# A 448-column first tile, one row for both signs, and a newly searched order in a fused Fourier and SwiGLU kernel

## The chip, the cores and the metric

The kernel runs on one core of a Trainium2 chip. The core has five engines that run side by side, each with its own queue of instructions: TensorE (PE, matrix products into the PSUM banks), VectorE (DVE) and ScalarE (ACT), which read and write PSUM and SBUF, GpSimd (POOL), which works on SBUF, and SyncE (SP), which here issues DMAs. They wait for each other by semaphores. The metric is the time of one execution in microseconds of device time. A profile shows one execution; its *span* runs from its first to its last instruction.

## The reference, cut to what matters

```python
def _attn_ref(x):                       # x: [8, 3008, 256]
    X = np.fft.fft(x, axis=1)           # along the sequence
    X = np.fft.fft(X, axis=2)           # along the features
    return X.real.astype(np.float32)

def _moe_ref(x, w_gate, w_val, w_out):  # x: [24064, 256]; w_gate, w_val: [256, 1536]; w_out: [1536, 256]
    g = x @ w_gate
    silu = g * (1.0 / (1.0 + np.exp(-g)))
    val = x @ w_val
    return (silu * val @ w_out).astype(np.float32)
```

The real part of a two-dimensional Fourier transform of each of eight batches is the token matrix of a gated feed-forward block: two projections to 1536 features, SiLU of the one times the other, and a projection back to 256.

## The kernel before, in words

**Pairs of rows.** Rows k and 3008 - k of a transformed batch share their cosine part P and have sine parts Q of opposite sign. So the kernel works on half the rows, 1504 columns for each of eight batches, 12,032 in all, and makes two results of each column: a *plus* value from P and Q, and a *minus* value with Q's sign turned. The eight rows 0, which have no partner, are eight more plus columns of the last tile. The transform along the features is folded into the weights: Wp and Wq are the weights for P and Q, and Wm is -2 Wq, so adding Wm times Q to a finished plus sum turns it into the minus sum.

**Tiles and units.** The columns are cut into 24 tiles (`wide`, line 41) of 512 columns, but for tiles 0 and 3 with 480 and the last with 320. T is 512, P is 128, H is 1504 columns a batch. A *unit* is a tile and one of twelve blocks of 128 of the 1536 features. `part_a` (line 1123) makes the plus sums of gate and value in PSUM banks g and v, `part_b` (line 1179), one unit later, the minus sums and the products. The plus product goes to the tile `hp`, the minus product to `hm` (`tiles_of`, line 1045), both bf16, the minus one in mirrored column order.

**Kinds.** `KINDS` (line 989) has one character for each unit, which says who does what. `w` is a whole unit: six matmuls, plus and minus sums from Wp, Wq and Wm, silus on ACT, both products on DVE; tile 0 has only these, since they need no prepared row. For the others the character is a hexadecimal number of flags. Without flags a unit has five matmuls: gate from Wp, Wq and Wm, value from Wp and Wq, and DVE makes the minus value as twice the even part less the plus sum. Flag 2 saves the gate's Wm matmul in the same way, for two more DVE instructions. Flag 1 lets ACT put the row-0 correction into the value bank ahead of time (a *seed*) and copy the even part, in place of a DVE instruction; that value then takes Wm as its last matmul. Flag 4 gives the plus product to POOL, whose instructions here read SBUF only, so ACT first copies the value to SBUF (`pp`, line 1250). Flag 8 gives POOL the minus value too (line 1256). The minus products of two units always go to POOL in one instruction (line 1244).

**Output blocks.** `OWork` (line 1269) multiplies the products of the tile before by Wo, in blocks of up to 128 columns: twelve matmuls for a block, one for each feature block, with the block as the weights that are loaded and the 256 columns of Wo streaming. Two blocks share a PSUM bank; ACT copies a pair to SBUF (`evict`), in one instruction where both have 128 rows and in two otherwise, and SP stores it, in as many pieces as the row order of the output asks for. Before the change the blocks of one sign are cut separately, so that a 480-column tile has blocks of 128, 128, 128 and 96 for each sign. The very last pair is evicted to an `es` buffer and stored from ACT's queue.

**Order.** Nothing runs in the order in which the program text makes it. Each operation goes to a planner (`Sched`, line 828) with an estimated duration, a due time on PE's own clock and the buffers that it takes and frees; the planner sets the order of every engine's queue before the kernel is built. The due time is shifted by `SHIFT` for each sort of operation and by `BIAS_ROWS` (line 778; the table above it is overwritten) for each tile and sort. The Fourier work of the next batches (folds on POOL, transform products on PE whose sums DVE writes to the tiles of P and Q) and of the weights (line 1519 with casts on ACT and DVE) is mixed in at fixed unit numbers, the main loop begins at line 1695.

Of the kernel before, what the change touches and what calls it, by code (L numbers as in the profile page):

```python
# [19 lines left out]
def kernel(  # L20
# [20 lines left out]
    wide = [H - 2 * T, T, T] * 2  # L41
# [674 lines left out]
    def rows(r0, n, step):  # L716
# [60 lines left out]
    )  # L777
    BIAS_ROWS = (
# [202 lines left out]
    def pool_us(n):  # L981
# [9 lines left out]
        "60ww24000310",  # L991
        "031310330010",
        "000031313300",
        "010210121013",
        "10110b103101",
        "031305121252",
        "401700014001",
        "331213050030",
        "010271031001",
        "33040b350300",  # L1000
        "01b300700101",
        "21302111b200",
        "001371310011",
        "23520011b212",
        "10130b130000",
        "031035003170",
        "013370040411",
        "303b21011210",
        "103b10219604",
        "0030b13300b0",  # L1010
        "616404563200",
        "143034169230",
        "704161632331",
# [31 lines left out]
    def tiles_of(t):  # L1045
        if t not in hts:
            hts[t] = (hp.tile([P, nF, T + B], BF16, name="hp"), hp.tile([P, nF, T], BF16, name="hm"))
        return hts[t]

# [73 lines left out]
    def part_a(u):  # L1123
# [9 lines left out]
        def h():  # L1133
            if t not in hts:
                hts[t] = (hp.tile([P, nF, T + B], BF16, name="hp"), hp.tile([P, nF, T], BF16, name="hm"))

# [42 lines left out]
    def part_b(u):  # L1179
# [15 lines left out]
        def sv():  # L1195
            if ksv not in T_:
                T_[ksv] = svp.tile([P, 2, T, 2], F32, name="sv")
            return T_[ksv]

        def hts_(t):  # L1200
            if t not in hts:
                hts[t] = (hp.tile([P, nF, T + B], BF16, name="hp"), hp.tile([P, nF, T], BF16, name="hm"))
            return hts[t]

        def g3():
            if by_dve:
                mm(T_[kg], Wq, 0, u, pq_tiles(t)[1], wp, False, True)
            else:
                mm(T_[kg], Wm, 0, u, pq_tiles(t)[1], w, False, True)

# [32 lines left out]
        def product_m():  # L1243
            nc.gpsimd.tensor_tensor(hts_(t)[1][:, f - 1:f + 1, :w], sv()[:, :, :w, 1], sv()[:, :, :w, 0], op=Alu.mult)  # L1244

        def product_p():
            nc.vector.tensor_tensor(hts_(t)[0][:, f, :wp], T_[ksp][:, :wp], T_[kv][:, :wp], op=Alu.mult)  # L1247
# [395 lines left out]
    def row_width(t):  # L1643
        return width(t) + (B if t == nT - 1 else 0)
# [138 lines left out]
```

## Time and profile before

| | |
|---|---|
| runs | 597.38, 598.56, 598.67 us; median 598.56 |
| profiled execution, span (the page gives no other time for it) | 596.2 us |
| PE busy | 590.3 us, 99% |
| DVE busy | 569.2 us, 95% |
| ACT busy | 553.6 us, 93% |
| POOL busy | 533.1 us, 89% |
| granted clock of PE | 1.000 |
| moved by DMA | 68.17 MB |

A row of a group reads: line, engine, operation, output<-inputs with shapes, count, then busy time, mean duration of one in ns, and the idle time of the engine just before with what ended it. A row of the timeline reads: start, duration, engine, line, what, count, and in brackets an idle time before it. A row of waits reads: who waited, for whom, total us, times, longest. Records of matmuls overlap, and those of ACT and DVE a little, so a duration can be longer than the distance between two starts. L1033 is the line of all gate and value matmuls, L1297 of the output matmuls.

### The profile page before, as it was taken

The page shows a single profiled execution, that of the slowest core. Times are in us where ns is not written, and L with a number is a line of the kernel's source. Part 1 is how long each engine was busy: PE and PEld are TensorE (multiplying, and loading weights), DVE is VectorE, ACT ScalarE, POOL GpSimd, SP SyncE. Part 2 cuts the span into 40 slices and gives each one's busy share as a digit, 9 for nine tenths or more (in the row PEclk, how much of TensorE's full clock was granted, in tenths as well). Part 3 has the DMA queues.
Part 4 walks back from the last instruction along what each step waited for, and adds up shares of the span by engine and source line. Part 5 has one row for each costly group of instructions (what it writes and reads, how often), then busy time and mean ns, then how long its engine had stood idle before and what let it go on. Part 6 is the DMA issues. An engine that isn't in the chain of part 4 may idle for free.

```text
span 596.2 us, 12375 instructions
## 1 busy us (share of the span) xinstructions
PE 590.3 (99%) x4001; PEld 388.7 (65%) x4001; DVE 569.2 (95%) x1063; ACT 553.6 (93%) x1071; POOL 533.1 (89%) x491
## 2 busy tenths in 40 slices
PE   8999999999999999999999999999999999999997
PEld 5456666666666666666666666666666666666686
DVE  8989999999999999999999999999999999999993
ACT  8768989999999899999999999999999999999995
POOL 8989999999999999999899998999889868687782
PEclk9999999999999999999999999999999999999999
DMA  8966772756243255275225122063121103202212
GB/s 244 166 219 234 189 230 71 195 165 220 83 151 126 70 144 132 54 254 165 81 79 171 37 63 64 19 182 113 47 63 37 47 19 89 66 29 63 60 54 81
DMA packets 61086, 68.17 MB, mean 114 GB/s; under 512 B 6760, under 2 KB 48684, under 8 KB 61022
## 3 DMA queue, kind: packets, MB, share of 16 engines
q1 hardware_dynamic: 57438, 64.44, 36.1%
q0 software_dynamic: 3216, 2.36, 2.8%
q8 instruction: 31, 0.51, 0.4%
q10 hardware_dynamic: 368, 0.59, 0.3%
q14 instruction: 33, 0.27, 0.1%
HBM read 40.21 MB, written 35.43 MB: 127 GB/s over the span
## 4 chain that ended last, share of the span: by engine, by line
PE 95%; DMA 1%; POOL 1%; SPq 1%; DVE 0%; ACT 0%; issue 0%; ACTq 0%; POOLq 0%
PE o L1297 40%; PE g L1033 27%; PE v L1033 21%; PE g L1471 2%; PE o L1471 2%; PE v L1297 1%; DMA XC<-in_x_dram 1%; DMA out_dram<-ev 1%; PE o L1519 1%; POOL t L373 0%; PE g L628 0%; PE o L628 0%; SPq L1310 0%; PE b L502 0%; PE b L490 0%
## 5 line engine op out<-in xcount | busy, mean ns | idle before, releaser
L1244 POOL TENSOR_TENSOR hm<-sv 128x1024 bf16<-128x1024 f32 (+2 forms) x137 | 254.7, 1862 | 32.7 <-ACT sv L1220 16.8
L1236 DVE SCALAR_TENSOR_TENSOR sv<-es,v 128x512 f32<-128x512 f32 (+2 forms) x262 | 174.5, 672 | 6.2 <-PE v L1033 4.3
L1297 PE MATMUL o<-Wo,hm 128*128 128x256 bf16 (+1 forms) x1128 | 163.7, 273 | 0.0
L1297 PE MATMUL o<-Wo,hp 128*128 128x256 bf16 (+1 forms) x1104 | 161.1, 272 | 0.0
L1247 DVE TENSOR_TENSOR hp<-sp,v 128x512 bf16<-128x512 f32 (+2 forms) x228 | 152.0, 673 | 1.8 <-PE v L1033 1.0
L1297 PEld LDWEIGHTS <-hm 128*128 128x128 bf16 (+2 forms) x1140 | 111.9, 98 | 58.0 <-issue 0.6
L1297 PEld LDWEIGHTS <-hp 128*128 128x128 bf16 (+2 forms) x1140 | 111.9, 98 | 55.4 <-issue 0.6
L1220 ACT ACTIVATE sv<-g 128x512 f32<-128x512 f32 (+2 forms) x181 | 118.4, 672 | 3.7 <-PE g L1033 3.2
L1145 ACT ACTIVATE sp<-g 128x512 f32<-128x512 f32 (+2 forms) x181 | 111.6, 618 | 6.1 <-PE g L1033 4.5
L1033 PE MATMUL g<-Pt,Wp 128*128 128x512 bf16 (+2 forms) x288 | 107.5, 374 | 0.0
L1033 PE MATMUL v<-Pt,Wp 128*128 128x512 bf16 (+2 forms) x288 | 106.2, 374 | 0.0
L1033 PE MATMUL g<-Qt,Wq 128*128 128x512 bf16 (+2 forms) x288 | 105.4, 375 | 0.0
L1106 ACT ACTIVATE v<-bc,w 128x512 f32<-128x512 bf16 (+2 forms) x139 | 99.7, 721 | 1.7 <-DVE sv L1236 0.9
L1170 DVE SCALAR_TENSOR_TENSOR es<-bc,w,v 128x512 f32<-128x512 bf16 (+2 forms) x135 | 98.1, 734 | 2.1
L1168 ACT ACTIVATE es<-v 128x512 f32<-128x512 f32 (+2 forms) x139 | 85.4, 617 | 3.3 <-PE v L1033 1.5
L1033 PE MATMUL g<-Qt,Wm 128*128 128x512 bf16 (+2 forms) x195 | 73.1, 376 | 0.0
L1033 PEld LDWEIGHTS <-Wp 128*128 128x128 bf16 x576 | 56.3, 98 | 25.2 <-issue 0.3
L1149 DVE SCALAR_TENSOR_TENSOR sg<-bc,w,g 128x512 f32<-128x512 bf16 (+2 forms) x93 | 67.5, 726 | 1.6 <-PE g L1033 1.4
L1253 POOL TENSOR_TENSOR hp<-sp,pp 128x512 bf16<-128x512 f32 (+1 forms) x46 | 57.1, 1245 | 8.0 <-ACT pp L1250 7.8
L1220 ACT ACTIVATE sv<-sg 128x512 f32<-128x512 f32 (+2 forms) x93 | 63.4, 693 | 0.5 <-POOL hp L1253 0.5
L1213 DVE SCALAR_TENSOR_TENSOR sg<-sg,g 128x512 f32<-128x512 f32 (+2 forms) x93 | 61.8, 665 | 0.2
L1033 PEld LDWEIGHTS <-Wq 128*128 128x128 bf16 x437 | 42.7, 98 | 28.4 <-issue 1.3
(201 smaller groups left out, 781.8 us busy)
## 6 DMA issues: line engine op xcount, KB each, us to landing
out_dram<-ev SPq DMA_DIRECT2D x96, 128.0 KB
XA<-in_x_dram SPq DMA_DIRECT2D x30, 256.0 KB
tA<-in_x_dram SPq DMA_DIRECT2D x28, 256.0 KB
XA<-tA SPq DMA_DIRECT2D x14, 512.0 KB
XC<-in_x_dram SPq DMA_DIRECT2D x28, 120.0 KB
tC<-in_x_dram SPq DMA_DIRECT2D x28, 120.0 KB
XC<-tC SPq DMA_DIRECT2D x6, 480.0 KB
bc<-br SPq DMA_DIRECT2D x19, 128.0 KB
```

What stands on the lines that cost most here:

```text
L1033: nc.tensor.matmul(ps[:, :n], Wt[:, gv, fs], src[:, :n], start=start, stop=stop, skip_group_check=True)
L1106: nc.scalar.activation(T_[kv][:, :w], bc[t][:, :w], AF.Copy, scale=w0[:, 1, f:f + 1])
L1145: nc.scalar.activation(sp_to()[:, :w], T_[kg][:, :w], AF.Silu)
L1149: nc.vector.scalar_tensor_tensor(T_[keg][:, :w], bc[t][:, :w], w0[:, 0, f:f + 1], T_[kg][:, :w], op0=Alu.mult, op1=Alu.add)
L1168: nc.scalar.activation(T_[kes][:, :w], T_[kv][:, :w], AF.Copy, scale=2.0 if on_pool(u) > 1 else 1.0)
L1170: nc.vector.scalar_tensor_tensor(T_[kes][:, :w], bc[t][:, :w], w0[:, 1, f:f + 1], T_[kv][:, :w], op0=Alu.mult, op1=Alu.add)
L1213: nc.vector.scalar_tensor_tensor(T_[kgm][:, :w], T_[keg][:, :w], 2.0, T_[kg][:, :w], op0=Alu.mult, op1=Alu.subtract)
L1220: nc.scalar.activation(sv()[:, f % 2, w - 1::-1, 1], T_[kgm if by_dve else kg][:, :w], AF.Silu)
L1236: nc.vector.scalar_tensor_tensor(sv()[:, f % 2, w - 1::-1, 0], T_[kes][:, :w], 2.0, T_[kv][:, :w], op0=Alu.mult, op1=Alu.subtract)
L1244: nc.gpsimd.tensor_tensor(hts_(t)[1][:, f - 1:f + 1, :w], sv()[:, :, :w, 1], sv()[:, :, :w, 0], op=Alu.mult)
L1247: nc.vector.tensor_tensor(hts_(t)[0][:, f, :wp], T_[ksp][:, :wp], T_[kv][:, :wp], op=Alu.mult)
L1297: nc.tensor.matmul(st["ps"][:n, j, :], hts[t][minus][:, f, c:c + n], Wo[:, f, :], start=(f == 0), stop=(f == nF - 1))
```

## The change

The first tile becomes 448 columns and all others but the last 512, so that tile 0 to 5 still cover two batches; the edge that was at column 1504, a batch's end, moves to 1472, and tile 3 now holds the last 32 columns of batch 0. Plus and minus products share one tile `h` of 1024 columns a feature block, the plus part first, and the minus part right behind it. Output blocks are cut over the whole row, so that a block can hold the end of the plus part and the start of the minus part; `stores` splits such a block by sign. A pair is evicted in two copies where one of its blocks is short, as before; in the last tile that is now the last pair, 128 and 8 rows. `KINDS` and `BIAS_ROWS` are replaced from the second tile on, the overwritten table is dropped, and three helpers that made the product tiles are merged into `tiles_of`.

```diff
-    wide = [H - 2 * T, T, T] * 2
+    wide = [2 * H - 5 * T] + [T] * 5
...
     BIAS_ROWS = (
         (8.55, -4.05, -3.45, 7.8, -31, -13.15, 16.6, 26.65, 26.15, 26.3, 26.75, 7.5, 3, 12.8, 13.35, -4.7, 4.55),
-        (-19.65, -7.75, -12.4, -1.6, -7, 5.65, -2.85, -2.85, 2.25, -3.5, 35.9, -0.75, -0.15, 1.9, -1.6, 3.8, -6.4),
...
+        (4.255, 1.638, -0.543, 4.143, -1.421, 1.089, -0.108, -0.795, -0.026, 0.763, 9.204, -7.067, -4.062, -1.119, -3.083, 5.491, -4.643),
...
     KINDS = (
         "wwwwwwwwwwww",
-        "60ww24000310",
-        "031310330010",
-        "000031313300",
-        "010210121013",
-        "10110b103101",
-        "031305121252",
-        "401700014001",
-        "331213050030",
-        "010271031001",
-        "33040b350300",
-        "01b300700101",
-        "21302111b200",
-        "001371310011",
-        "23520011b212",
-        "10130b130000",
-        "031035003170",
-        "013370040411",
-        "303b21011210",
-        "103b10219604",
-        "0030b13300b0",
-        "616404563200",
-        "143034169230",
-        "704161632331",
+        "20ww00001101",
+        "213013443211",
+        "013031130101",
+        "123010311010",
+        "131000950001",
+        "213103111213",
+        "012145214301",
+        "031772700001",
+        "301071033010",
+        "312154035212",
+        "503310b00011",
+        "329271130301",
+        "211044001071",
+        "630307142030",
+        "112147034000",
+        "039603903301",
+        "301013560400",
+        "377601444303",
+        "1b00592b7004",
+        "00922150b630",
+        "644b24124920",
+        "7073400b6000",
+        "70b27724b220",
     )
...
     def tiles_of(t):
         if t not in hts:
-            hts[t] = (hp.tile([P, nF, T + B], BF16, name="hp"), hp.tile([P, nF, T], BF16, name="hm"))
+            h = hp.tile([P, nF, 2 * T], BF16, name="h")
+            w = row_width(t)
+            hts[t] = (h[:, :, 0:w], h[:, :, w:w + width(t)], h)
         return hts[t]
+
+    def row_width(t):
+        return width(t) + (B if t == nT - 1 else 0)
...
             w = width(t)
-            blocks = []
-            for minus in (0, 1):
-                n = w + (B if (t == nT - 1 and not minus) else 0)
-                for c in range(0, n, P):
-                    blocks.append((minus, c, min(P, n - c)))
+            wp = row_width(t)
+            blocks = [(c, min(P, wp + w - c)) for c in range(0, wp + w, P)]
...
-            nc.tensor.matmul(st["ps"][:n, j, :], hts[t][minus][:, f, c:c + n], Wo[:, f, :],
+            nc.tensor.matmul(st["ps"][:n, j, :], hts[t][2][:, f, c:c + n], Wo[:, f, :],
                              start=(f == 0), stop=(f == nF - 1))
...
         def stores(self, pair, t):
-            return [(jj, p0, cnt, r0, step) for jj, (mi, cc, nn) in enumerate(pair)
-                    for p0, cnt, r0, step in row_pieces(t0[t] + (width(t) - cc - nn if mi else cc), nn, mi)]
+            w, wp = width(t), row_width(t)
+            res = []
+            for jj, (c, n) in enumerate(pair):
+                for lo, hi, minus in ((c, min(c + n, wp), 0), (max(c, wp), c + n, 1)):
+                    if lo < hi:
+                        first = wp + w - hi if minus else lo
+                        res += [(jj, lo - c + p0, cnt, r0, step) for p0, cnt, r0, step in row_pieces(t0[t] + first, hi - lo, minus)]
+            return res
```

Counted in the instruction orders of the two kernels, the totals over all tiles go as follows.

| | before | after |
|---|---|---|
| gate and value matmuls | 1361 | 1357 |
| output matmuls | 2280 | 2268 |
| units with flag 2 (gate split) | 93 | 97 |
| units with flag 1 (seed) | 139 | 137 |
| plus products on POOL | 46 | 67 |
| minus values on POOL | 12 | 15 |
| store issues on SP / ACT | 278 / 1 | 280 / 2 |

More of the change, by code (lines that the diff above doesn't have):

```diff
@@ L752 @@
     BIAS_ROWS = (
[24 rows of a table removed]
-    )
-    BIAS_ROWS = (
[24 rows of a table removed]
[24 rows of a table added]
     )
@@ L1131, in part_a @@
         kb = (("bc", t), 0)
-        def h():
-            if t not in hts:
-                hts[t] = (hp.tile([P, nF, T + B], BF16, name="hp"), hp.tile([P, nF, T], BF16, name="hm"))
         def g1():
@@ L1198, in sv @@
             return T_[ksv]
[L1200 to L1203, printed above, removed]
         def g3():
@@ L1243, in product_m @@
         def product_m():
-            nc.gpsimd.tensor_tensor(hts_(t)[1][:, f - 1:f + 1, :w], sv()[:, :, :w, 1], sv()[:, :, :w, 0], op=Alu.mult)
+            nc.gpsimd.tensor_tensor(tiles_of(t)[1][:, f - 1:f + 1, :w], sv()[:, :, :w, 1], sv()[:, :, :w, 0], op=Alu.mult)
         def product_p():
-            nc.vector.tensor_tensor(hts_(t)[0][:, f, :wp], T_[ksp][:, :wp], T_[kv][:, :wp], op=Alu.mult)
+            nc.vector.tensor_tensor(tiles_of(t)[0][:, f, :wp], T_[ksp][:, :wp], T_[kv][:, :wp], op=Alu.mult)
         def value():
@@ L1252, in product_g @@
         def product_g():
-            nc.gpsimd.tensor_tensor(hts_(t)[0][:, f, :wp], T_[ksp][:, :wp], pair_of(u)[:, :wp], op=Alu.mult)
+            nc.gpsimd.tensor_tensor(tiles_of(t)[0][:, f, :wp], T_[ksp][:, :wp], pair_of(u)[:, :wp], op=Alu.mult)
         def mirror_g():
@@ L1282, in __init__ @@
                 pair = blocks[i:i + 2]
-                if len(pair) == 2 and pair[0][0] != pair[1][0]:
-                    pair = pair[:1]
                 i += len(pair)
@@ L1289, in __init__, with product @@
                     st.update(home=(esp, "es"), queue=nc.scalar)
-                for j, (minus, c, n) in enumerate(pair):
+                for j, (c, n) in enumerate(pair):
                     for f in range(nF):
-                        self.steps.append((st, pair, j, minus, c, n, f, t))
-        def product(self, st, pair, j, minus, c, n, f, t):
+                        self.steps.append((st, pair, j, c, n, f, t))
+        def product(self, st, pair, j, c, n, f, t):
             if "ps" not in st:
                 st["ps"] = st["pool"].tile([P, 2, D], F32, name=st["nm"])
-            nc.tensor.matmul(st["ps"][:n, j, :], hts[t][minus][:, f, c:c + n], Wo[:, f, :],
+            nc.tensor.matmul(st["ps"][:n, j, :], hts[t][2][:, f, c:c + n], Wo[:, f, :],
                              start=(f == 0), stop=(f == nF - 1))
@@ L1302, in evict @@
             st["ev"] = ev = home.tile([P, T], F32, name=nm).rearrange("p (j d) -> p j d", j=2)
-            if all(q[2] == P for q in pair):
+            if all(q[1] == P for q in pair):
                 nc.scalar.copy(ev[:, 0:len(pair), :], st["ps"][:, 0:len(pair), :])
@@ L1306, in evict @@
                 for jj, q in enumerate(pair):
-                    nc.scalar.copy(ev[:q[2], jj, :], st["ps"][:q[2], jj, :])
+                    nc.scalar.copy(ev[:q[1], jj, :], st["ps"][:q[1], jj, :])
         def store(self, st, jj, p0, cnt, r0, step):
@@ L1321, in run @@
                 todo = todo[len(grp):]
-                st, pair, _, _, _, _, _, t = grp[0]
+                st, pair, _, _, _, _, t = grp[0]
                 ko = ((st["nm"], ("out", st["id"])), 0)
                 S.add("PE", pe_us(D) * len(grp), lambda grp=grp: [self.product(*s) for s in grp],
-                      r=[(("h", t), ("pm"[s[3]], s[6])) for s in grp] + ([] if t else [(("Wo",), 0)]), w=[ko], new=[ko[0]])
-                if grp[-1][2] == len(pair) - 1 and grp[-1][6] == nF - 1:
+                      r=[(("h", t), (k, s[5])) for s in grp for k in "p" * (s[3] < row_width(t)) + "m" * (s[3] + s[4] > row_width(t))] + ([] if t else [(("Wo",), 0)]), w=[ko], new=[ko[0]])
+                if grp[-1][2] == len(pair) - 1 and grp[-1][5] == nF - 1:
                     ke = ((st["home"][1], ("out", st["id"])), 0)
@@ L1641 @@
     before.setdefault(SIGN_AT, []).append(signed_op)
-    def row_width(t):
-        return width(t) + (B if t == nT - 1 else 0)
     def first_rows16(t):
```

68 rows, old and new, of the table BIAS_ROWS are left out of this document.

## The prediction

> **What bounds the kernel now.** I read the page first, then the list of waits for TensorE (PE) alone, then stretches of time, then short pieces of the timeline.
>
> ```profile
> span 596.2 us, 12375 instructions
> PE 590.3 (99%) x4001; PEld 388.7 (65%) x4001; DVE 569.2 (95%) x1063; ACT 553.6 (93%) x1071; POOL 533.1 (89%) x491
> PE 95%; DMA 1%; POOL 1%; SPq 1%; DVE 0%; ACT 0%; issue 0%; ACTq 0%; POOLq 0%
> ```
>
> PE is busy 99% of the span and carries 95% of the chain that ended last. The other three are close behind, so a busy share alone does not settle it. The waits of PE do, and the stretch between its first and its last dense matmul:
>
> ```profile
> PE b L314 <- DVE sel L263: 1.0, 1, 1.0
> PE v L1033 <- DVE hp L1071: 0.5, 1, 0.5
> PE b L490 <- DVE EOf L460: 0.4, 1, 0.4
> PE b L485 <- ACT EOb L497: 0.2, 1, 0.2
> ...
> 22.00:592.60 570.60, 570.55 (x3896) 378.25 (x3894) 549.21 (x988) 535.96 (x1041) 513.28 (x446) 1.00 0.38 111
> 592.60:596.20 3.60, 0.02 (x1) 0.00 (x0) 0.00 (x0) 0.36 (x1) 0.00 (x0) 0.94 0.31 91
> ```
>
> Columns of the last two rows: length, then PE, weight loads, DVE, ACT, POOL with their instructions, granted clock, DMA share, GB/s. After 22 us PE has no wait that the list names, is busy 570.55 of 570.60 us, and the clock is 1.00. So the time is a head of some 22 us, PE's matmuls laid end to end, and a tail of 3.6 us. A busy record overlaps the next one, though; what a matmul costs is the distance between starts:
>
> ```profile
> 301.73 0.38 PE L1033 MATMUL g<-Qt,Wm 128*128 128x512 bf16 x1
> ...
> 302.59 0.60 PE L1297 MATMUL o<-Wo,hm 128*128 128x256 bf16 x4
> 303.03 0.38 PE L1033 MATMUL g<-Qt,Wm 128*128 128x512 bf16 x1
> ```
>
> Four 512-column matmuls start between 301.73 and 302.59: 0.86/4 = 0.215 us each, not the 0.38 of the record. Four 256-column ones take 0.44/4 = 0.110. That is 0.41 ns a column and 5 ns fixed, so 480 columns cost 0.202, 448 cost 0.189, and 320 or 328 about 0.137. An output matmul streams the 256 columns of Wo however few rows its block has: a block of 8 rows costs 0.110 a step too.
>
> **The change, part by part.**
>
> *Matmuls.* The first tile has 72 gate and value matmuls in both kernels (twelve units of six): 480 to 448 columns saves 72 x 0.013 = 0.96 us. Tile 3 goes from 56 matmuls of 480 columns (11.33 us) to 57 of 512 (12.29): +0.96. These two cancel; the columns only move. In the other full tiles the new kinds have 3 matmuls fewer (-0.65), in the last tile 2 of 320 columns fewer (-0.27). Output blocks: tile 0 had four blocks for each sign (128, 128, 128, 96 rows) and now has seven full ones over 896 columns; tile 3 keeps eight, the last tile six. One block of twelve steps goes: -12 x 0.110 = -1.31. PE sum: -2.2 us. All of it lies on the path, since PE has no gap to absorb it.
>
> *Head.* Here the new order has a price. The planner now puts the cast of a weight chunk (Wp, L1522) on DVE ahead of the first product of tile 0, and the PE instruction that adds Wm to the value bank of unit 0 has to wait for that product:
>
> ```profile
> 21.12 1.21 DVE L1071 TENSOR_TENSOR hp<-sg,v 128x480 bf16<-128x480 f32 x2
> 22.25 0.68 DVE L1522 CAST Wp<-o 128x512 bf16<-128x512 f32 x1
> 22.85 0.40 DVE L377 SCALAR_TENSOR_TENSOR XA<-EOf,mM,XA 128x188 f32<-128x188 f32 x1
> ...
> 18.26 0.57 PE L1033 MATMUL g<-Pt,Wp 128*128 128x480 bf16 x2
> 20.95 0.37 PE L1033 MATMUL g<-Pt,Wp 128*128 128x480 bf16 x1
> 21.81 0.36 PE L1033 MATMUL v<-Qt,Wm 128*128 128x480 bf16 x1 [0.50 <-DVE hp L1071]
> ```
>
> Before: the product starts at 21.12 and PE resumes at 21.81, 0.66 us after 20.95 + 0.20. After: DVE is free at 21.12 as before, the cast takes 22.85 - 22.25 = 0.60, the 448-wide product 0.61, so PE resumes near 22.37. By then it has issued eleven matmuls of 448 and four of 512 columns since 18.26 (2.94 us, to 21.20): a stall of 1.17 in place of 0.66, **+0.5**. The queue behind it is all of PE's. I carried the next four units on by hand with the same rows, and each later wait (for the bank that a minus product frees) is met before PE gets there, so the 0.5 is paid once. Bounds: 0, if the later waits of this stretch shrink in return, and 0.6, the whole cast.
>
> *Tail.* Before, the last block has 64 rows: one copy, one store. After, the last pair is a full block and an 8-row block, copied one after the other, then two stores on ACT's queue.
>
> ```profile
> 592.66 0.36 ACT L1307 COPY es<-g 64x256 f32<-64x256 f32 x1 [0.80 <-PE g L1297]
> 593.05 0.56 ACTq L1310 DMA_DIRECT2D out_dram<-es  x1
> 52.94 0.64 ACT L1307 COPY ev<-o 128x256 f32<-128x256 f32 x2 [1.23 <-PE o L1297]
> L1310 SPq DMA_DIRECT2D out_dram<-ev x278: 254/360/1249, 49.0 to 592.3; - x139
> ```
>
> Two such copies take 0.64 where one takes 0.36, so the second ends 0.27 later; a store issue costs 0.36 in the median. If the first issue runs beside the second copy, only one issue is added (0.36); if it waits for it, both (0.63). I take **+0.4**, nearer the first, because each store waits for its own copy and the copy is the shorter of the two. Below, 0: what ends the span is the landing, 2.6 us after the issue ends at 593.61, and an 8-row store might land sooner.
>
> *DVE, ACT, POOL.* Units that leave the plus product to POOL rise by 21 (46 to 67); each needs a copy on ACT. POOL also makes three more mirror values.
>
> ```profile
> L1253 POOL TENSOR_TENSOR hp<-sp,pp 128x512 bf16<-128x512 f32 x42 | 53.6, 1279 | 7.1 <-ACT pp L1250 6.9
> L1247 DVE TENSOR_TENSOR hp<-sp,v 128x512 bf16<-128x512 f32 x208 | 140.4, 681 | 1.7 <-PE v L1033 1.0 <-ACT sv L1220 0.2
> L1250 ACT COPY pp<-v 128x512 f32<-128x512 f32 x42 | 25.6, 610 | 0.9 <-DVE sv L1236 0.8
> L1244 POOL TENSOR_TENSOR hm<-sv 128x1024 bf16<-128x1024 f32 x125 | 236.5, 1894 | 29.2 <-ACT sv L1220 13.3 <-DVE sv L1236 9.6 <-issue 2.1
> L1244 POOL TENSOR_TENSOR hm<-sv 128x960 bf16<-128x960 f32 x6 | 10.7, 1785 | 0.0
> ```
>
> POOL gains 19 x 1.28 + 2 x 0.89 for the products and 3.0 for the mirrors: about +29 us, to 562. ACT gains some 11 (mostly 21 copies of 0.61 or less), to 564; DVE loses 9, to 560. With PE's 2.2 off, all three stay below some 594 of span. Cost taken: 0, hidden under PE, while POOL's waits in the last row but one (29.2 us, mostly for work of ACT and DVE) shrink. If that cover goes, the excess is PE's; see the rivals. In the merged row a minus product writes two separate runs of 512 rather than one of 1024; the 480-wide tiles already do that at 1785/960 = 1.86 ns an element against 1894/1024 = 1.85, so it costs nothing.
>
> *Stores, puts, gathered code.* SP issues 280 stores where it issued 278, at 0.36 us each beside PE; ACT one more (counted above). Moving a tile edge to column 1472 splits two more transform outputs: two 32-wide adds on DVE, inside its 9 us of relief. Searched offsets reorder every engine but add no work; what stalls they leave after the head I set equal to before's.
>
> **Sum.** -2.2 + 0.5 + 0.4 = -1.3 us. Span 596.2 becomes 594.9. The page gives the span only; the three runs, 597.38 to 598.67, lie 1.2 to 2.5 above it, and from their median 598.56 the forecast is **597.3**.
>
> **Rivals.**
>
> *POOL becomes the bound (slower).* Place: a stretch in which POOL has no idle time to give.
>
> ```profile
> 60.00:100.00 40.00, 40.00 (x276) 26.74 (x274) 39.34 (x75) 36.08 (x71) 39.83 (x39) 1.00 0.58 169
> 100.00:160.00 60.00, 60.00 (x411) 40.11 (x410) 57.61 (x105) 57.60 (x113) 59.22 (x55) 1.00 0.58 170
> ...
> 400.00:460.00 60.00, 60.00 (x413) 40.02 (x412) 57.95 (x106) 58.19 (x111) 52.14 (x44) 1.00 0.26 80
> ```
>
> POOL idles 0.2 us of 40 and 0.8 of 60 between 60 and 160 us, but 7.9 of 60 after 400. Tiles 2 to 5, which run there, get four POOL products where there was one: 3 x 1.28 = 3.8 us more into 1.0 of idle. A pair of minus products has two buffers, so a late one holds up ACT and DVE, and then PE's banks. The surplus of 2.8 would be PE's: 597.3 + 2.8 = **600.1**. It decides from 2.5 us of lost PE time on (the line of 0.2% above 598.56). For it: the two rows. Against it: tile 1 gives two POOL products up just before (-2.6), and most of the new ones sit late (tiles 16 to 23: 40 against 26), where the idle is.
>
> The Trainium skill, GPSIMD Engine Reference, section 4.1 Engine selection, says elementwise work belongs on VectorE, as GpSimd is about twice as slow with two inputs. This trace agrees on the price (1279 against 681 ns). By that rule the moved products are the wrong way round, which is this rival with its 600.1; by PE's own stretch a slower engine costs nothing as long as PE does not wait for it.
>
> *The new order also removes the little stalls (faster).* PE's stretch after 22 us has holes too short for the list of waits:
>
> ```profile
> 260.02 0.38 PE L1033 MATMUL g<-Qt,Wq 128*128 128x512 bf16 x1
> 260.45 0.38 PE L1033 MATMUL v<-Qt,Wm 128*128 128x512 bf16 x1
> ...
> 255.64 3.57 DMA out_dram<-ev
> 259.31 0.04 ACT ev L1304
> 259.79 0.61 ACT es L1168
> ```
>
> The starts lie 0.43 apart instead of 0.215; the chain leads back to a store of 3.57 us that freed a buffer late. With some five like it I estimate 1 us in all. If those go and the head's 0.5 comes back: -2.2 - 1.0 + 0.4 = -2.8, **595.8**.
>
> *The gain is spent (no change).* The offsets were searched anew; holes of 0.1 to 0.2 us in ten places take 1.3 us back: **598.5**.
>
> **How the numbers follow.** Chances: forecast 0.40 (own range 596.5 to 598.2), faster rival 0.25, POOL 0.20, spent 0.15. A measurement tells 0.2% (1.2 us) from no change. The forecast lies just beyond that line: 0.24 of its 0.40 counts as faster, 0.14 as same, 0.02 slower. With the faster rival (0.25) and a little of the spent case (0.03): faster 0.52. Same: 0.14 + 0.11 = 0.25. Slower: 0.02 + 0.01 + 0.20 = 0.23. The range goes down to 595.2 (the faster rival with the tail hidden) and up to 600.6 (POOL, and 0.5 for a second hole of that kind).
>
> **What would show it.** Right: 2268 output matmuls, PE's list of waits headed by a DVE product at some 1.2 us in tile 0, a last ACT store issue about 0.4 later after PE's end than before, POOL near 562 us busy with PE unwaiting. Wrong: PE rows waiting on POOL's h, or ACT and DVE rows waiting on POOL for 1 us and more in tiles 2 to 5; or gaps between PE starts that add up to more than 1 us behind 22 us.

## The result, and the profile after

| | before | after |
|---|---|---|
| median of 9 runs each, us | 598.12 | 599.47 |
| lowest to highest, us | 597.38 to 598.67 | 599.18 to 600.50 |
| span of the profiled execution, us | 596.2 | 597.0 |

The ratio is 1.0026, with a 95% interval of 1.0017 to 1.0036: the change makes the kernel 0.26% slower, where the prediction had it 0.2% faster. These are the first rows of the page of the changed kernel (span, busy time, the chain that ended last):

```profile
span 597.0 us, 12297 instructions
PE 586.7 (98%) x3925; PEld 386.1 (65%) x3985; DVE 563.8 (94%) x1051; ACT 560.2 (94%) x1084; POOL 561.4 (94%) x515
PE 83%; POOL 6%; DVE 4%; issue 3%; DMA 2%; ACT 2%; SPq 0%; DVEq 0%; ACTq 0%; POOLq 0%
```

POOL's busy time is as foretold (562); ACT, foretold as 564, and DVE, as 560, are each some 4 us off. The chain has changed more: PE carried 95% of it before and carries 83% now, and POOL, DVE, ACT and DMAs have most of the rest. Now the head of the list of waits for PE:

```profile
PE b L314 <- DVE sel L263: 1.0, 1, 1.0
PE v L1007 <- POOL XA L373: 1.0, 1, 1.0
PE v L1007 <- DVE h L1217: 0.8, 2, 0.6
```

The third row is new and lies behind the head, where PE had no listed wait before.

*How the delays are counted.* Where nothing waits, the starts of matmuls of n columns lie (n + 6)/2400 us apart in these traces: 0.216 for 512, 0.189 for 448 and 0.109 for 256, within 0.001 of the prediction's prices. (The 24 matmuls of one column at 31 us start some 0.03 apart and are counted so.) Summed in the order in which they stand on PE, from the first gate matmul on, the matmuls of the kernel before cost 571.06 us and those of the changed one 568.84. What a matmul starts later than this sum says is delay. In the changed kernel 60 of 3985 matmul records are missing (the weight loads, PEld, are complete). A missing record looks like a hole of one matmul, so records are matched with the instruction order before a hole is counted. The table below is good to about 0.1 us for the one execution that each row shows; executions of one kernel differ by more, those of the changed one from 599.18 to 600.50.

| delay gathered, us | to 30 us | 30–60 | 60–90 | 90–150 | 150–210 | 210–270 | 270–end | sum |
|---|---|---|---|---|---|---|---|---|
| before | 0.77 | 0.30 | 0.10 | 0.26 | 0.04 | 0.65 | 1.02 | 3.14 |
| after | 1.23 | 0.68 | 0.77 | 0.65 | 0.39 | 1.15 | 1.10 | 5.97 |

So the 2.2 us of matmuls were saved, and 2.83 us of delay took their place. The three largest places in the trace are these. First, the head (rows picked out of the timeline of the changed kernel):

```profile
18.41 0.54 PE L1007 MATMUL g<-Pt,Wp 128*128 128x448 bf16 x2
21.27 0.68 DVE L1493 CAST Wp<-o 128x512 bf16<-128x512 f32 x1
21.87 1.13 DVE L1050 TENSOR_TENSOR h<-sg,v 128x448 bf16<-128x448 f32 x2
21.19 0.35 PE L1007 MATMUL g<-Qt,Wq 128*128 128x448 bf16 x1
22.52 0.35 PE L1007 MATMUL v<-Qt,Wm 128*128 128x448 bf16 x1 [0.98 <-POOL XA L373]
```

The cast stands ahead of the products, the first product ends near 22.48 and PE goes on at 22.52, 1.14 us late. The row puts the wait down to a POOL instruction that ends at the same 22.52; the experiment that moves the cast will tell which of the two it is.

Second, tile 2. POOL makes a fold and then a minus product; ACT and DVE wait for the buffer that this product frees, and PE waits for DVE:

```profile
70.17 2.36 POOL L187 TENSOR_TENSOR SDf<-XA 128x1020 f32<-128x1020 f32 x1
72.64 1.90 POOL L1214 TENSOR_TENSOR h<-sv 128x1024 bf16<-128x1024 f32 x1
74.56 0.65 ACT L1190 ACTIVATE sv<-g 128x512 f32<-128x512 f32 x1 [0.41 <-POOL h L1214]
74.57 0.69 DVE L1206 SCALAR_TENSOR_TENSOR sv<-es,v 128x512 f32<-128x512 f32 x1 [0.62 <-POOL h L1214]
75.91 0.38 PE L1007 MATMUL v<-Pt,Wp 128*128 128x512 bf16 x1 [0.27 <-DVE h L1217]
```

Third, tile 9. Its row 0, which DVE needs in all partitions (`bc`), leaves SP's queue at 230.34, behind a train of loads of x and two stores, and DVE waits for it. In the kernel before it left ahead of the same train, at 208.28 (first row):

```profile
208.28 0.56 SPq L1659 DMA_DIRECT2D bc<-br  x1
...
225.03 3.56 SPq L169 DMA_DIRECT2D XC<-in_x_dram  x4
230.34 0.61 SPq L1627 DMA_DIRECT2D bc<-br  x1
233.99 0.75 DVE L1124 SCALAR_TENSOR_TENSOR sg<-bc,w,g 128x512 f32<-128x512 bf16 x1 [0.92 <-DMA bc<-br]
236.59 0.38 PE L1007 MATMUL v<-Pt,Wp 128*128 128x512 bf16 x1 [0.56 <-DVE h L1217]
```

PE loses 0.73 us there and 0.29 at 238.

One more part lies outside the span. The time less the span is 1.72 to 1.85 us in the runs of the kernel before and 2.18 to 2.27 in those of the changed one: some 0.43 us that no row of the profile shows.

### The profile page after: what moved, and what is told of

Read it like the earlier page. It is cut to its first block, busy times and chain, and to the rows that moved or that the text cites. A ratio compares the mean times of both kernels' runs of the same rounds, so it can differ in the third digit from the quotient of the medians.

```text
span 597.0 us, 12297 instructions
## 1 busy us (share of the span) xinstructions
PE 586.7 (98%) x3925; PEld 386.1 (65%) x3985; DVE 563.8 (94%) x1051; ACT 560.2 (94%) x1084; POOL 561.4 (94%) x515
## 4 chain that ended last, share of the span: by engine, by line
PE 83%; POOL 6%; DVE 4%; issue 3%; DMA 2%; ACT 2%; SPq 0%; DVEq 0%; ACTq 0%; POOLq 0%
PE o L1262 36%; PE g L1007 22%; PE v L1007 19%; PE g L1442 2%; PE o L1442 2%; POOL h L1214 1%; DVE h L1217 1%; DVE sv L1206 1%; DMA tC<-in_x_dram 1%; DMA tA<-in_x_dram 1%; DMA bc<-br 1%; DVE es L1145 1%; ACT es L1143 1%; POOL SDf L187 0%; POOL XA L403 0%
## 5 line engine op out<-in xcount | busy, mean ns | idle before, releaser
L1262 PE MATMUL o<-Wo,h 128*128 128x256 bf16 x2220 | 321.5, 272 | 1.0
L1262 PEld LDWEIGHTS <-h 128*128 128x128 bf16 x2268 | 221.4, 98 | 113.7 <-issue 2.2
L1214 POOL TENSOR_TENSOR h<-sv 128x1024 bf16<-128x1024 f32 (+1 forms) x137 | 255.8, 1870 | 15.8 <-ACT sv L1190 7.8
L1206 DVE SCALAR_TENSOR_TENSOR sv<-es,v 128x512 f32<-128x512 f32 (+1 forms) x259 | 174.0, 677 | 10.7 <-PE v L1007 8.8
L1217 DVE TENSOR_TENSOR h<-sp,v 128x512 bf16<-128x512 f32 (+1 forms) x207 | 138.6, 678 | 2.5 <-PE v L1007 1.7
L1190 ACT ACTIVATE sv<-g 128x512 f32<-128x512 f32 (+1 forms) x177 | 117.4, 682 | 3.5 <-PE g L1007 1.8
L1120 ACT ACTIVATE sp<-g 128x512 f32<-128x512 f32 (+1 forms) x177 | 109.3, 625 | 4.1 <-DVE h L1217 1.9
L1145 DVE SCALAR_TENSOR_TENSOR es<-bc,w,v 128x512 f32<-128x512 bf16 (+1 forms) x137 | 99.8, 735 | 3.0 <-PE v L1007 0.7
L1085 ACT ACTIVATE v<-bc,w 128x512 f32<-128x512 bf16 (+1 forms) x137 | 98.2, 724 | 1.6 <-DVE sv L1206 0.7
L1143 ACT ACTIVATE es<-v 128x512 f32<-128x512 f32 (+1 forms) x137 | 84.8, 622 | 2.8 <-PE v L1007 1.0
L1187 ACT ACTIVATE sp<-g 128x512 f32<-128x512 f32 (+1 forms) x97 | 58.2, 600 | 1.4 <-DVE sg L1183 1.3
```

Source lines behind the costliest of these rows:

```text
L1085: nc.scalar.activation(T_[kv][:, :w], bc[t][:, :w], AF.Copy, scale=w0[:, 1, f:f + 1])
L1120: nc.scalar.activation(sp_to()[:, :w], T_[kg][:, :w], AF.Silu)
L1143: nc.scalar.activation(T_[kes][:, :w], T_[kv][:, :w], AF.Copy, scale=2.0 if on_pool(u) > 1 else 1.0)
L1145: nc.vector.scalar_tensor_tensor(T_[kes][:, :w], bc[t][:, :w], w0[:, 1, f:f + 1], T_[kv][:, :w], op0=Alu.mult, op1=Alu.add)
L1190: nc.scalar.activation(sv()[:, f % 2, w - 1::-1, 1], T_[kgm if by_dve else kg][:, :w], AF.Silu)
L1206: nc.vector.scalar_tensor_tensor(sv()[:, f % 2, w - 1::-1, 0], T_[kes][:, :w], 2.0, T_[kv][:, :w], op0=Alu.mult, op1=Alu.subtract)
```

## The experiments

Two theories at first. *Order*: the delays come from the newly searched kinds and offsets. *Structure*: the merged row and the blocks that span both signs hold PE up. Each time is given with its ratio, and 95% interval, to the kernel before on the same chip, whose medians lay between 597.70 and 598.03 us.

**Old kinds and offsets on the new structure, and the reverse**

The first kernel is the changed one with both tables, `BIAS_ROWS` and `KINDS`, of the kernel before; the second is the reverse. The beginning of the first edit:

```diff
     KINDS = (
         "wwwwwwwwwwww",
-        "20ww00001101",
-        "213013443211",
+        "60ww24000310",
+        "031310330010",
...
```

> The new structure (448-wide first tile, one row for both signs) with the kinds and offsets of the kernel before. If the lost time is the new order's (theory: order), the matmuls are 12 output steps of 0.110 us fewer than before (-1.3), the delays that PE gathers beyond its matmuls laid end to end fall from 6.0 back to some 3.1 us, and the time is near 596.8. If the merged row itself holds PE up (rival: structure), the delays stay near 6 and the time is 599 or more.

> The old structure with the new kinds and offsets. Order theory: matmuls 0.9 us less than before, delays near 6 us as in the changed kernel, so about 600.0. Structure rival: delays near 3.1, so about 597.2.

Measured: 603.53 us (ratio 1.0096, 1.0080 to 1.0111) and 605.54 us (1.0139, 1.0109 to 1.0169), with delays of 10.4 and 10.6 us. Both expectations missed. The first gathers 3.55 us between 210 and 270 us, the second 7.1 us after 270. An order is good for the structure for which it was searched, and either half of the change alone is worse than the whole.

**The merged row alone, and the widths alone**

The row alone is the changed kernel with widths, kinds and offsets of the kernel before; the widths alone are this line in the kernel before:

```diff
-    wide = [H - 2 * T, T, T] * 2
+    wide = [2 * H - 5 * T] + [T] * 5
```

> The kernel before with only the merged row for both signs (480-wide tiles, kinds and offsets as before, 2280 output matmuls as before). DVE's order does not change, the other engines' only around the output blocks. If the merged row costs nothing (order theory), the time is that of the kernel before, 597.7, and PE's delays beyond its matmuls stay near 3.1 us. If it holds PE up (structure rival), the delays grow by 2 us or more and the time is 599.5 or more.

> The kernel before with only the tile widths changed (448 and then 512), rows, kinds and offsets as before, 2280 output matmuls. Order theory: the offsets were searched for other unit times, so delays of several us come up as with old tables on the whole new structure: about 602 to 604. Structure rival, with the row as the culprit: about 597.7.

Measured: the row alone 599.05 us (1.0014, 1.0005 to 1.0022), delays 4.0; the widths alone 605.13 us (1.0118, 1.0105 to 1.0131), delays 10.6. The widths go the way of the order theory, which had 602 to 604. The row alone costs 0.9 us of delay, which neither theory had. It sits in two tiles, at 61.9 to 64.7 and 133.4 to 136.8 us. Here is the timeline of the row alone, and then the same place of the kernel before:

```profile
61.91 0.62 PE L1262 MATMUL o<-Wo,h 128*64 128x256 bf16 x4
62.47 0.39 PE L1007 MATMUL g<-Qt,Wm 128*128 128x512 bf16 x1
62.70 0.38 PE L1007 MATMUL v<-Qt,Wm 128*128 128x512 bf16 x1
63.01 0.62 PE L1262 MATMUL o<-Wo,h 128*64 128x256 bf16 x4
```

```profile
61.85 0.60 PE L1297 MATMUL o<-Wo,hm 128*96 128x256 bf16 x4
62.28 0.38 PE L1033 MATMUL g<-Qt,Wm 128*128 128x512 bf16 x1
```

A merged row of 960 columns ends in a block of 64, where the separate signs ended in blocks of 96. Four matmuls with 96 weight columns take 0.43 us to the next start; with 64 they take 0.56, and the start of such a group is late by 0.09 as well (62.70 + 0.216 = 62.92, but 63.01). Going from 128 to 64 weight columns and back costs 0.22 us for a group; the six groups in two tiles gather 1.35 us, and elsewhere this kernel is some 0.4 us below the kernel before, most of it between 210 and 270 us. The Trainium skill, TensorEngine Tiling (Array Packing), section Tiling Modes, says that changing the tiling mode drains TensorE; it gives no price. These rows fit that, though they show only the lost time and not a drain as such. The changed kernel's 448-wide tile has 896 = 7 x 128 columns in a row and no such block, so this is not where its delay is from: as far as the row goes, the structure theory falls. That the new structure does not need the delays of the changed kernel is shown by the kernel with POOL relieved, below, which has it and gathers 3.6 us (3.14 in the kernel before).

**One instruction moved: the cast behind the products**

The next three kernels are the changed kernel with its finished order edited just before it is built; all else stays.

```diff
+            o = op("DVE", (("Wp",), (1, 0)))
+            order.remove(o)
+            order.insert(order.index(op("DVE", (("h", 0), ("p", 1)))) + 1, o)
```

> The changed kernel with one instruction moved in the finished order: the cast of the weight chunk on DVE goes behind the first two products of tile 0. Order theory: PE resumes near 21.9 us in place of 22.52, the stall there falls from 1.14 to about 0.55, and 0.6 us come off: 598.9. Rival: later waits of tile 0 take the gain back and the time stays at 599.5.

Measured: 599.02 us (1.0022, 1.0011 to 1.0034). The stall fell from 1.14 to 0.55, as expected, so the cast was the cause of what the new order had added to it. The delay to 30 us fell by less, from 1.23 to 0.89, since PE now loses 0.19 us a little later, at 22.98. That of 60 to 90 us rose from 0.77 to 1.75, and the time can't be told from the changed kernel's. Some waits of PE in this kernel, and a row of POOL's timeline:

```profile
PE v L1013 <- DVE h L1223: 0.9, 2, 0.7
PE g L1013 <- ACT sv L1196: 0.7, 1, 0.7
PE v L1013 <- DVE h L1056: 0.4, 1, 0.4
```

```profile
39.93 2.35 POOL L187 TENSOR_TENSOR SDf<-XC 128x1020 f32<-128x1020 f32 x1 [3.81 <-DMA XC<-tC]
```

The head's wait is down to 0.4 listed, and one of 0.7 has come up, at 75 us. POOL's fold began 1.0 us later than in the changed kernel (38.90), after a load, so this run does not say by itself how much of the gain POOL would have taken back.

**The row of tile 9 earlier**

```diff
+            o = op("SP", (("bc", 9), 0))
+            sp = [x for x in order if x.eng == "SP"]
+            ahead = sp[sp.index(o) - 15]
+            order.remove(o)
+            order.insert(order.index(ahead), o)
```

> The changed kernel with one DMA moved in the finished order: on SP's queue the row that tile 9 needs in all partitions goes ahead of the 15 planned loads and stores in front of it. Order theory: DVE no longer waits 0.9 us for it at 233 us, PE's holes of 0.73 and 0.29 us at 235 to 239 us go, and the time is near 598.5. Rival: the holes come from POOL and stay, 599.5.

Measured: 598.01 us (1.0004, 0.9994 to 1.0013). In this kernel the row is issued ten us earlier and DVE takes it with no wait:

```profile
219.90 0.60 SPq L1635 DMA_DIRECT2D bc<-br  x1
232.78 0.74 DVE L1132 SCALAR_TENSOR_TENSOR sg<-bc,w,g 128x512 f32<-128x512 bf16 x1
```

The delay of 210 to 270 us fell from 1.15 to 0.30, the whole from 5.97 to 5.01. One DMA behind the wrong neighbours had cost some 1 us.

**The fold behind the minus product, and all three moves**

```diff
+            o = op("POOL", (("h", 2), ("m", 0)))
+            folds = [x for x in order if x.eng == "POOL" and (("fold",), "F") in x.w and order.index(x) < order.index(o)]
+            order.remove(folds[-1])
+            order.insert(order.index(o) + 1, folds[-1])
```

> The changed kernel with one fold of 2.4 us on POOL moved behind the minus product that stood after it (tile 2, 70 us). Order theory: that product ends 2.4 us earlier, ACT and DVE do not wait for its buffer at 74.5 us, PE's holes at 74.7 to 77 us (0.6 in all) go, 598.9. Rival: POOL has no idle time there, so the hole only moves on: 599.5.

> All three moves in the changed kernel: cast behind the products, row of tile 9 earlier, fold behind the minus product. Order theory: head 0.55, tile 2 0.6 and tile 9 1.0 to 1.4 come off 599.47: 597.1. Rival (POOL is the bound from 54 to 75 us and takes the head's gain back): as with the row alone, 598.0.

Measured: 599.17 us (1.0018, 1.0009 to 1.0027) and 598.00 us (1.0003, 0.9995 to 1.0012). The fold's place made nothing of tile 2's delay: 0.77 us with the fold moved alone, 0.84 with all three. The hole went from 75 on to 79 us. The chain of waits of the kernel with three moves says why; its first and last pieces on POOL, and what follows:

```profile
47.39 1.89 POOL h L1229
...
76.16 1.86 POOL h L1229
78.05 0.64 ACT sv L1205
78.69 0.57 ACT v L1100
79.26 0.04 issue
79.30 0.59 PE v L1022 x2
```

Between 47.4 and 78 us the chain does not leave POOL and its queue. Whatever stands in which place, POOL has some 30 us of work in a row there. The time is that of the row alone, as the rival had it. In the trace, though, tile 2 did not take the head's gain back: the delay fell from 5.01 to 4.40, and tiles 2 and 3 begin 0.5 us earlier than in the changed kernel (63.32 against 63.86 and 88.42 against 88.88).

**Take work from POOL**

```diff
     def halve_tables():
-        nc.gpsimd.memset(Tab[0:64, 1, :, :, GH + 1:NCE], 0.0)
-        nc.gpsimd.memset(Tab[64:P, 1, :, :, 0:GH + 1], 0.0)
+        nc.vector.memset(Tab[0:64, 1, :, :, GH + 1:NCE], 0.0)
+        nc.vector.memset(Tab[64:P, 1, :, :, 0:GH + 1], 0.0)
```

This was done to the changed kernel alone, with the cast (behind the first product) and the row moved, and with the fold moved too.

> The changed kernel with 1.46 us of POOL's work taken away: the two fills with zeros at 51 us go to DVE, in the same place of the finished order. POOL theory (POOL is the bound from 47 to 78 us, so each us taken from it is PE's, up to the 0.77 us that PE gathers there): PE's delays between 60 and 90 us fall from 0.77 to 0.1 us, time near 598.8. Rival (DVE or ACT set the pace there, DVE is now 1 us fuller): the delays stay or grow, 599.5 or more.

> The changed kernel with the cast behind the first product of tile 0 (not behind the first two), the row of tile 9 earlier and the fills with zeros on DVE. POOL theory: the head's 0.55 is no longer lost in tile 2, so head 0.55, tile 2 0.7, tile 9 1.0 come off 599.47: 597.2. Rival: 598.0, as with the three moves before.

> As the run before, with the fold of tile 2 moved behind the minus product as well. POOL theory: with POOL relieved the place of the fold matters little, within 0.3 us of the run before (about 597.2). Rival: the fold is what holds tile 2 up, and only this one loses the holes there: 0.7 us less than the run before.

Measured: 599.42 us (1.0026, 1.0015 to 1.0038), 598.29 (1.0007, 0.9998 to 1.0016) and 598.39 (1.0009, 1.0001 to 1.0018). In all three the delay of 60 to 90 us fell from 0.77 to 0.14 or less. That speaks for POOL but does not settle it, since in all three PE was held up by 1.4 us at 54 us and came later to tile 2; the next kernel is without that. The new order itself had brought part of POOL's work into the stretch. This is the first of the two fills in the kernel before, in front of the full stretch, and in the changed kernel, in it:

```profile
35.72 0.72 POOL L1617 MEMSET Tab<- 64x752 bf16 x1
...
50.88 0.72 POOL L1588 MEMSET Tab<- 64x752 bf16 x1
```

Their place alone does not make the delay: the old structure with the new tables has the first fill at 50.74 us as well and gathers 0.04 us between 60 and 90. The times all missed what the POOL theory had (598.8, 597.2 and 597.2), for DVE got the work, and the timeline of the first of the three shows the price:

```profile
51.96 0.69 DVE L1588 MEMSET Tab<- 64x752 bf16 x1
52.84 0.69 DVE L1589 MEMSET Tab<- 64x756 bf16 x1 [0.20 <-issue]
53.56 0.69 DVE L1071 TENSOR_TENSOR h<-sg,v 128x512 bf16<-128x512 f32 x1
54.30 0.38 PE L1007 MATMUL v<-Pt,Wp 128*128 128x512 bf16 x1 [1.25 <-DVE h L1071]
```

DVE has no room at 52 us either: two fills and 0.2 us between them put off a product by 1.6 us, and PE waited 1.25. So the time of the first did not move. The place of the fold made 0.1 us between the other two, as the POOL theory had it.

**Take work from POOL where another engine has room**

With the cast and the row moved as above:

```diff
+            odds = [o for o in order if (("Tab",), "k") in o.w]
+            order.remove(odds[1])
+            order.insert(order.index(op("ACT", (("od", (0, 1, 1)), 0))) + 1, odds[1])
+            o = op("POOL", (("Tab",), "z"))
+            order.remove(o)
+            order.insert(order.index(odds[3]) + 1, o)
...
     def odd_table(c, half):
...
-        nc.gpsimd.tensor_copy(Tab[r, c, :, :, NCE:NCE + GH], src[:, :, ::-1] if half else src)
+        copy = nc.scalar.copy if (c, half) == (0, 1) else nc.gpsimd.tensor_copy
+        copy(Tab[r, c, :, :, NCE:NCE + GH], src[:, :, ::-1] if half else src)
```

> The changed kernel with cast and row moved, and POOL relieved where another engine has room: of the four table copies of 0.81 us one goes to ACT, which idles at 39 to 40.6 us, and the fills with zeros move up to the last copy, where POOL waits for PE; the minus product at 47.9 us starts on time. POOL theory: tile 2's 0.77 goes without DVE's 1.41 at 54 us coming in its place, PE's delays end near 3.6 us (6.0 in the changed kernel), the time is near 597.0. Rival (the engines are so full that any relief comes back elsewhere): 598.0 or more.

Measured: **596.78 us**, ratio 0.9986 (0.9977 to 0.9995) to the kernel before. The copy lies in an idle stretch of ACT, and the fills in the stretch in which POOL had waited for PE, ahead of the product that starts at 47.9 as before. From the timeline:

```profile
38.58 0.83 ACT L1612 COPY Tab<-Tab 64x752 bf16<-64x752 bf16 x1
46.34 0.72 POOL L1605 MEMSET Tab<- 64x752 bf16 x1
47.10 0.73 POOL L1606 MEMSET Tab<- 64x756 bf16 x1
47.91 1.89 POOL L1231 TENSOR_TENSOR h<-sv 128x1024 bf16<-128x1024 f32 x1
```

Waits of PE, and the chain that ended last:

```profile
PE b L314 <- DVE sel L263: 1.0, 1, 1.0
PE v L1024 <- DVE h L1067: 0.4, 1, 0.4
PE b L485 <- ACT EOb L497: 0.2, 1, 0.2
```

```profile
PE 92%; ACT 2%; DVE 2%; issue 2%; POOL 1%; DMA 1%; ACTq 0%; DVEq 0%; POOLq 0%
```

The list names no wait of PE behind the head, and POOL is down from 6% of the chain to 1%. The delay of 60 to 90 us is 0.08 with no new one ahead of it (0.52 from 30 to 60), and PE comes to tile 2 earlier than in the changed kernel, at 63.09 against 63.86: tile 2's delay was POOL's. The delays of the edited kernels in one table, one execution each. Four kernels that leave tile 9's row where it was (after, cast, fold, fills to DVE) lie between 0.90 and 1.22 from 210 to 270 us, so differences of 0.3 us between two rows say nothing by themselves. In all of them the table leaves out the 0.09 us that PE loses on the way into its last block, of 8 rows; in the kernel before the like is counted, for its last block of 64:

| delay gathered, us | to 30 us | 30–60 | 60–90 | 90–150 | 150–210 | 210–270 | 270–end | sum |
|---|---|---|---|---|---|---|---|---|
| after | 1.23 | 0.68 | 0.77 | 0.65 | 0.39 | 1.15 | 1.10 | 5.97 |
| cast | 0.89 | 0.61 | 1.75 | 0.56 | 0.39 | 1.22 | 0.99 | 6.41 |
| row of tile 9 | 1.32 | 0.57 | 0.85 | 0.64 | 0.35 | 0.30 | 0.98 | 5.01 |
| fold | 1.33 | 0.58 | 0.77 | 0.66 | 0.33 | 0.91 | 1.02 | 5.60 |
| cast, row, fold | 0.88 | 0.61 | 0.84 | 0.63 | 0.35 | 0.12 | 0.97 | 4.40 |
| fills to DVE | 1.25 | 2.09 | 0.10 | 0.55 | 0.41 | 0.90 | 1.43 | 6.73 |
| cast, row, POOL relieved | 0.97 | 0.52 | 0.08 | 0.58 | 0.33 | 0.15 | 0.95 | 3.58 |

**What lies outside the span**

The time less the span is steady for each kernel to 0.1 us, but not the same for all: 1.8 us (medians) for the kernel before, its row-only and widths-only forms and the new structure with old tables, 2.0 for the old structure with new tables and for the three with fills on DVE, 2.1 for the one with POOL relieved, 2.2 for the changed kernel and its first four edits. The changed kernel has 24 more instructions on POOL, so that was tried on the kernel before:

```diff
+            late = [o for o in order if o.eng == "POOL"][-60::2]
...
                 o.fn()
+                if o in late:
+                    nc.gpsimd.memset(turn_sign[:, 0:1], 0.0)
```

> The kernel before with 30 one-column fills on POOL added among its last 60 operations, where POOL idles. If the time outside the span (1.8 us in the kernel before, 2.2 in the changed one) goes with the number of POOL's instructions, it rises to 2.2 here; if not, it stays at 1.8. The span stays within 0.5 us.

Measured: 597.66 us (1.0002, 0.9992 to 1.0012), 1.76 outside the span. It is not the count of POOL's instructions. What it is stays open.

## Why the prediction was wrong, step by step

The prediction was 597.3, faster; measured were 599.47, slower, though within the outer bounds of 595.2 and 600.6, which the rivals had set. (Its lower bound is 0.2 too low by its own terms: 598.56 less 2.8 and 0.4 is 595.4.)

- **What bounds the kernel:** right for the span: nearly all that came or went in it is PE's work or PE's delay.
- **Matmuls, -2.2:** right, 571.06 to 568.84. The experiments show that it is there to be had: with the delays back at 3.6 the kernel is faster than before.
- **Head, +0.5:** right in place, cause and size (0.46). What the step missed is that most of it can be undone by moving one instruction.
- **Tail, +0.4:** wrong in size, it is -0.05, at its low bound of 0. From the start of the last copy to the end of the span it is 3.54 us before (592.66 to 596.2) and 3.49 after:

```profile
593.51 0.63 ACT L1272 COPY es<-g 128x256 f32<-128x256 f32 x2 [1.21 <-PE g L1262]
593.91 0.98 ACTq L1275 DMA_DIRECT2D out_dram<-es  x2
```

  The first store is issued 0.40 us after its copy starts, as before (0.39); the second store is issued some 0.4 later, as the step had it, but the span does not end later for it; which landing ends the span was not taken apart.
- **DVE, ACT and POOL, cost 0, and the stalls set equal:** this step failed. POOL's busy time came out as worked out, and so did the price of each POOL product (1.28); ACT gained 6.6 us and not 11, DVE lost 5.4 and not 9. What failed is the sentence on the searched offsets, "what stalls they leave after the head I set equal to before's": a term put at nothing, with no row behind it. These stalls are 4.74 us (5.97 - 1.23) against 2.37 (3.14 - 0.77): +2.4, more than the whole gain. Two places stand out: tile 2 (+0.67) and tile 9 (+1.02 between 210 and 240 us); the stalls near 260 us that the kernel before had went from 0.62 to 0.10 and gave 0.5 back. The experiments show what the two places hang on: the row's place in SP's queue, and POOL's work in its full stretch. The rest, 0.35 to 0.39 us each in 30 to 60, 90 to 150 and 150 to 210 us, lies in holes of 0.05 to 0.25 us that were not taken apart; their cause stays open.
- **Stores, puts, SP's queue:** counted by number and price only. The step costed what SP issues more, and not what the new order puts ahead of the row of tile 9. That was the largest single place.
- **From span to time:** the sum took the time outside the span as unchanged. It grew by 0.43 us, a third of what was measured; the cause is open.
- **The rival of POOL:** its mechanism was there, and its condition (no idle time on POOL between 60 and 160 us) was read from the right rows. Its price was 0.7 and not 2.8, and its cause was not the one given: tile 1 has no plus product on POOL, and those of tile 2 come behind the hole. POOL was already full there in the kernel before (24.83 of 25 us between 65 and 90), and the new order moved the two fills (1.45 us) into its stretch. PE also reaches tile 2 earlier, at 63.86 against 64.02. Without the fills there the kernel with POOL relieved has no delay, though PE comes earlier still; with the fills, but with tile 2 at 64.32, the old structure with the new tables has next to none. So the fills and an early PE seem to be needed together, but no run varies PE's arrival alone.
- **The rival of the spent gain** described the rest best (many small holes), with 1.3 us where it was 2.4 with the two large places.
- **The signs of being wrong:** one was met by the kernel before already, whose gaps behind the head add up to 2.37 us; it could not have told the two apart. The waits for POOL in tile 2 are there (0.8 us of ACT and 0.6 of DVE).

The sum: -2.22 matmuls, +0.46 head, +2.37 other delay, -0.05 tail. The main stream began 0.15 later (18.41 against 18.26), which is scatter: over all kernels run here it began between 18.07 and 18.67, with no rule. Some 0.1 us more is the way into the 8-row block, which the table leaves out. That makes +0.8 of span, as measured; with 0.43 outside it, +1.2, against +1.35 in the medians (0.17% to 0.36%, so 1.0 to 2.2).

The Trainium skill, GPSIMD Engine Reference, section 4.1 Engine selection, has elementwise add, multiply and max on VectorE. It does not speak of fills, and no run here moved the products back. The fills moved to DVE took 1.45 us from POOL and put 1.4 us of delay on PE through DVE, and the time stayed; ACT and an idle stretch of POOL itself were the place. With all four engines some 94% busy or more, the idle time of an engine at that spot decided here, and not its speed (0.69 us for a fill on DVE, 0.72 on POOL).

## What to carry to other kernels

When an order is made anew, don't set its stalls equal to the old one's: price the stretches where a second engine has no idle time left, because work that the new order puts there can come out as a delay of PE. Look at each in-order queue, DMA issues included, for a load with a deadline behind loads without one. An order that was searched fits one structure, so change the structure with the search, and look at the finished order by hand: two moved entries, one copy on another engine and a pair of fills moved up were worth 0.4% here (1.0026 to 0.9986 of the kernel before), more than the change itself had cost. Such a move gains only where the engine that gets the work idles at that spot: the same fills on DVE gained nothing.

## What the runs showed of the hardware that was not expected

- A group of matmuls with 64 weight columns between groups with 128 costs PE 0.22 us, 0.09 of it ahead of the group; 96 columns cost nothing.
- A load of x in the train above holds SP's queue for 0.89 us (3.56/4), where a store takes 0.36 in the median, so such a train puts off what is behind it by more than its number tells.
- A bf16 fill of 64 x 752 takes 0.69 us on DVE and 0.72 on POOL, and a copy of that size 0.83 on ACT and 0.81 on POOL: for these, the engine makes a difference of 0.03 us at most.
- The time outside the profiled span differs between kernels, 1.8 to 2.2 us, and is steady to 0.1 us within each.
